# First batch computed in step with the weight loads over four output accumulators, with a second PSUM layout for the rest

## The chip, the cores and the metric

The kernel runs on one core of one Trainium2 chip. The metric is the time of one execution in device microseconds (us). Two spans appear: the time that a run reports, and the span of its trace, from the first to the last instruction, some 2 us shorter. Each run also has a mean granted TensorE clock, where 1.0 is full speed.

Most runs of the kernel before agree within one per cent. Runs carry a state, fast or slow; for one core "slow" means over 1.5% above the fastest run of the same kernel.

## The reference, cut to what matters

```python
B, H, S, Ns, D = (8, 8, 512, 32, 64)          # x: B,H,S,D   state: B,H,Ns,D
scores = scale * x @ state^T ; a = softmax(scores) ; xread = a @ state
scores2 = scale * state @ x^T ; a2 = softmax(scores2) ; sread = a2 @ x
y = concat([xread, sread], axis=2)            # per batch 512 + 32 rows
y = y.transpose(0, 2, 1, 3).reshape(B * 544, 512)
h = y @ w_in                                   # 512 -> 2048
out = (0.5 * h * (1 + erf(h / sqrt(2)))) @ w_out   # 2048 -> 512
```

There are eight batches. The kernel never forms `xread`: it multiplies the small `state` with `w_in` first (`pmat`), and then the transposed attention weights with that product (`mm1`).

## The kernel before: the parts that matter here

Engines run their own instruction lists, each in the order in which the kernel records them (e1 and e8 below show it: moving two recorded calls took back 15 us, and a product recorded behind sixteen load issues on POOL ran 11.5 us after its operand was ready). PE is TensorE (matmuls), DVE the vector engine, ACT the scalar engine, POOL the GpSimd engine (it also issues the large loads). Of PSUM, where matmuls write, the kernel uses eight banks: six for work in progress and two as accumulators, each of which gathers one output tile over several steps until DVE copies it out.

```python
ps_f = tile_pool(name="ps_f", bufs=6, space=PSUM)   # six banks of work
ps_o = tile_pool(name="ps_o", bufs=2, space=PSUM)   # two output accumulators
# loads on the POOL queue, in this order:
#   w_in 0, w_in 1, state 1..7, x 1, w_in 2, w_in 3, w_out 0, w_out 1, x 2, w_out 2, w_out 3, x 3

def norm(b, half):                   # softmax weights of a half batch: all on DVE
    nc.vector.reduce_sum(out=cs, in_=e4)        # waits for the Exp on ACT
    nc.vector.reciprocal(out=ics, in_=cs)
    nc.vector.tensor_tensor(out=A.a[...], in0=e4, in1=ics, op=mult)

def mm1(b, m):                       # first layer, one of 16 tiles of a batch
    hp = ps_f.tile([128, 512]); 2 matmuls (attention^T, P)
    nc.scalar.activation(out=gs[b][:, m, :], in_=hp, func=Gelu)

def evac(ps, rows):                  # accumulator -> SBUF -> HBM
    nc.vector.tensor_copy(out=osb, in_=ps)
    nc.sync.dma_start(out=rows, in_=osb)

def mm2(u):                          # second layer: a unit is 4 matmuls, 16 units per batch
    b, r = u // 16, u % 16
    if b == 0:  j, q = 2 * (r // 8) + r % 2, (r % 8) // 2     # two tiles side by side
    else:       j, q = r // 4, r % 4                          # one tile after the other
    if q == 0:  ops[j % 2] = ps_o.tile(...)
    4 matmuls (g of hidden blocks 4q..4q+3, w_out) added to the accumulator
    if q == 3:  evac(...)

def steady(b):                       # what is done for the next batch nb, by step s
    d[0] = begin, rearr, load_x, xtr(nb, 0) ; d[1] = xtr(nb, 1)
    d[3] = scores(nb, 0), scores(nb, 1), norm(nb, 0), norm(nb, 1)
    d[7] = pmat(nb, (0, 1)) ; d[9] = atr ; d[11], d[12] = sread ; d[13] = pmat ; d[14] = srt

lag = 16
for b in range(B):
    for s in range(16):
        for f in plan.get(s, ()): f()
        mm1(b, s); done += 1
        if done > lag: mm2(u); u += 1
```

`xtr` transposes x, `scores` makes the logits and their Exp, `atr` transposes the attention weights, `sread` and `srt` make the reads of the state rows.

The softmax here doesn't subtract the row's maximum and nothing guards it: scores larger than these inputs give would overflow.

Of the kernel before, what the change touches and what calls it, by code (L numbers as in the profile page):

```python
# [9 lines left out]
FP32 = mybir.dt.float32  # L10
# [7 lines left out]
def kernel(  # L18
# [8 lines left out]
    nc = tc.nc  # L27
# [13 lines left out]
    att = ctx.enter_context(tc.tile_pool(name="att", bufs=2))  # L41
    gpool = ctx.enter_context(tc.tile_pool(name="gpool", bufs=3))
    opool = ctx.enter_context(tc.tile_pool(name="opool", bufs=4))
    ps_f = ctx.enter_context(tc.tile_pool(name="ps_f", bufs=6, space=bass.MemoryType.PSUM))
    ps_o = ctx.enter_context(tc.tile_pool(name="ps_o", bufs=2, space=bass.MemoryType.PSUM))

    ctx.enter_context(tc.manual_schedule())



# [8 lines left out]
    st_f = persist.tile([128, 2, D], FP32, name="st_f")  # L59
    st_bf = persist.tile([128, B, 2, D], BF16, name="st_bf")  # L60
    x0f = persist.tile([128, 2, HC, SJ * D], FP32, name="x0f")
    warm = persist.tile([128, 512], BF16, name="warm")
    x4s = [persist.tile([128, SJ, HC, 132], BF16, name=f"x4_{i}") for i in range(2)]

# [2 lines left out]
    x0_rows = x[0].rearrange("(t c) (p j) d -> p t c (j d)", t=2, j=SJ)  # L67
    nc.scalar.dma_start(out=st_f, in_=st_rows[:, 0, :, :])
    for c in range(HC):
        eng = nc.sync if c % 2 == 0 else nc.scalar  # L70
        eng.dma_start(out=x0f[:, :, c, :], in_=x0_rows[:, :, c, :])

    make_identity(nc, ident)
    nc.vector.memset(warm, 0.0)  # L74
# [5 lines left out]
    def load_w_in(f):  # L80
        for t in range(2):
            nc.gpsimd.dma_start(
                out=w_in_bf[64 * t:64 * t + 64, :, f * 512:(f + 1) * 512],
                in_=moe_w_in[256 * t:256 * t + 256, f * 512:(f + 1) * 512].rearrange(
                    "(c d) f -> d c f", c=HC
                ),
            )
# [3 lines left out]
    def load_w_out(i):  # L91
        nc.gpsimd.dma_start(out=w_out_bf[:, 4 * i:4 * i + 4, :], in_=w_out_r[:, 4 * i:4 * i + 4, :])
# [3 lines left out]
    def load_x(b):  # L96
        xb = xin.tile([128, H, SJ * D], BF16, name="xb", tag="xb")
        nc.gpsimd.dma_start(out=xb, in_=x[b].rearrange("h (p j) d -> p h (j d)", j=SJ))
        xbs[b] = xb

    load_w_in(0)
    load_w_in(1)
    nc.gpsimd.dma_start(
        out=st_bf[:, 1:B, :, :].rearrange("q b t d -> q (b t) d"),
        in_=st_rows[:, 1:B, :, :].rearrange("q b t d -> q (b t) d"),
    )
    load_x(1)
    load_w_in(2)
    load_w_in(3)
    load_w_out(0)  # L110
    load_w_out(1)
    load_x(2)
    load_w_out(2)
    load_w_out(3)
    load_x(3)


    def keep_warm(n):
# [61 lines left out]
    def xtr0(c):  # L180
        A = atts[0]
        ps = ps_f.tile([128, SJ, 128], BF16, name="xT_ps", tag="f")
        for j in range(SJ):
            nc.tensor.transpose(ps[:, j, :], A.x4[:, j, c, 2:130], ident)
        nc.scalar.copy(out=A.xT[:, c, :, :], in_=ps)

    def xtr(b, half):
        A = atts[b]
# [6 lines left out]
    def score_mms(b, c):  # L195
        A = atts[b]
        if c % 2 == 0:
            A.pt = ps_f.tile([128, SJ, 2, 2, NS], FP32, name="pt", tag="f")
        for j in range(SJ):
            nc.tensor.matmul(  # L200
                A.pt[:, j, :, c % 2, :],
                lhsT=A.xT[:, c, j, :],
                rhs=sbd[:, b, c, :],
                start=True,
                stop=True,
            )
# [10 lines left out]
    def scores(b, half):  # L217
        score_mms(b, 2 * half)
        score_mms(b, 2 * half + 1)
        expo(b, half)  # L220

    def norm(b, half):
        A = atts[b]
        G = SJ * 2
        hs = slice(64 * half, 64 * half + 64)
        e4 = A.e[:, :, hs].rearrange("p g (c n) -> p g c n", n=NS)
        cs = att.tile([128, G, 2], FP32, name="cs", tag="cs")
        nc.vector.reduce_sum(out=cs, in_=e4, axis=AX.X)  # L228
        ics = att.tile([128, G, 2], FP32, name="ics", tag="ics")
        nc.vector.reciprocal(out=ics, in_=cs)  # L230
        nc.vector.tensor_tensor(  # L231
            out=A.a[:, :, hs].rearrange("p g (c n) -> p g c n", n=NS),
            in0=e4,
            in1=ics[:, :, :].to_broadcast((128, G, 2, NS)),
            op=ALU.mult,
        )
# [61 lines left out]
    def pmat(b, fs, act=()):  # L298
        if b not in Ps:
            Ps[b] = att.tile([128, 2, d_ff], BF16, name="P", tag="P")  # L300
        pss = []
        for f in fs:
            ps = [ps_f.tile([128, 512], FP32, name="p_ps", tag="f") for t in range(2)]
            for c in range(HC):
                for t in range(2):
                    nc.tensor.matmul(  # L306
                        ps[t][32 * c:32 * c + 32, :],
                        lhsT=sbd[64 * t:64 * t + 64, b, c, 32 * t:32 * t + 32],
                        rhs=w_in_bf[64 * t:64 * t + 64, c, f * 512:(f + 1) * 512],
                        start=True,  # L310
                        stop=True,
                    )
            pss.append(ps)
        for f, ps in zip(fs, pss):
            for t in range(2):
                dst = Ps[b][:, t, f * 512:(f + 1) * 512]
                if (f, t) in act:
                    nc.scalar.copy(out=dst, in_=ps[t])  # L318
                else:
                    nc.vector.tensor_copy(out=dst, in_=ps[t])  # L320
# [20 lines left out]
    def evac(ps, rows, last=False):  # L341
        osb = opool.tile([128, d_model], FP32, name="osb", tag="osb")
        if last:
            h = d_model // 2
            nc.vector.tensor_copy(out=osb[:, 0:h], in_=ps[:, 0:h])
            nc.sync.dma_start(out=rows[0][0][:, 0:h], in_=osb[:, 0:h])
            nc.scalar.copy(out=osb[:, h:], in_=ps[:, h:])
            nc.scalar.dma_start(out=rows[0][0][:, h:], in_=osb[:, h:])
            return
        nc.vector.tensor_copy(out=osb, in_=ps)  # L350
        for r, src in rows:
            nc.sync.dma_start(out=r, in_=osb[src, :])

    def mm2(u):
        b, r = u // 16, u % 16
        if b == 0:
            j, q = 2 * (r // 8) + r % 2, (r % 8) // 2
        else:
            j, q = r // 4, r % 4
        if q == 0:  # L360
            ops[j % 2] = ps_o.tile([128, d_model], FP32, name="op", tag="op")
        ps = ops[j % 2]
        for m in range(4 * q, 4 * q + 4):
            nc.tensor.matmul(  # L364
                ps,
                lhsT=gs[b][:, m, j * 128:(j + 1) * 128],
                rhs=w_out_bf[:, m, :],
                start=(m == 0),
                stop=(m == MC - 1),
            )  # L370
        if q == 3:
            rows = out[b * SB:b * SB + S, :].rearrange("(p j) n -> j p n", j=SJ)[j]
            evac(ps, [(rows, slice(0, 128))], last=(u == 16 * B - 1))

    def mm1_sr(m):
        hp = ps_f.tile([128, B * NS], FP32, name="hps", tag="f")
# [30 lines left out]
    for c in range(HC):  # L407
# [6 lines left out]
    expo(0, 0)  # L414
    xtr0(3)
    score_mms(0, 2)
    keep_warm(2)
    score_mms(0, 3)
    expo(0, 1)
    norm(0, 0)  # L420
    norm(0, 1)
    keep_warm(6)
    pmat(0, (0,), act=((0, 0), (0, 1)))
    keep_warm(4)
    atr(0)
    keep_warm(2)

    extra = {
        0: {
            1: [lambda: pmat(0, (1,))],  # L430
            3: [lambda: state_prep(1, B)],
            5: [lambda: begin(1), lambda: rearr(1), lambda: xtr(1, 0)],
            6: [lambda: xtr(1, 1), lambda: scores(1, 0), lambda: scores(1, 1)],
            7: [lambda: pmat(0, (2,))],
            8: [lambda: norm(1, 0), lambda: norm(1, 1)],
            10: [lambda: pmat(0, (3,))],
            12: [lambda: pmat(1, (0,))],
            13: [lambda: atr(1)],
            14: [lambda: pmat(1, (1,))],
        },  # L440
        1: {
            0: [lambda: sread(0, 0)],
            1: [lambda: sread(0, 1), lambda: pmat(1, (2,))],
            2: [lambda: srt(0)],
            3: [lambda: pmat(1, (3,))],
            4: [lambda: sread(1, 0)],
            5: [lambda: sread(1, 1), lambda: begin(2), lambda: rearr(2), lambda: load_x(4), lambda: xtr(2, 0)],
            6: [lambda: xtr(2, 1), lambda: srt(1)],
            8: [lambda: scores(2, 0), lambda: scores(2, 1), lambda: norm(2, 0), lambda: norm(2, 1)],
            10: [lambda: pmat(2, (0, 1), act=((0, 1), (1, 1)))],  # L450
            12: [lambda: atr(2)],
            13: [lambda: sread(2, 0)],
# [26 lines left out]
        d[14] = [lambda: srt(nb)]  # L479
        return d  # L480

    u = 0
    lag = 16
    done = 0
    for b in range(B):
        plan = extra[b] if b in extra else steady(b)
        for s in range(MC):
            for f in plan.get(s, ()):
                f()
            mm1(b, s)  # L490
            done += 1
            if done > lag:
                mm2(u)
                u += 1
# [40 lines left out]
```

## Time and profile before

| | before |
|---|---|
| time, median of 4 runs | 241.5 us (240.62 to 242.85) |
| span of the trace | 238.6 us |
| first `mm1`, first Gelu, first `mm2` | 14.73, 16.37, 31.91 us |
| period of one batch from batch 3 on (start of `srT` to start of `srT`) | 24.87 us |

The page of the kernel before. The first two lines are the span and the busy time of each engine with its share; then PE's busy tenths and its granted clock in 40 slices of 6 us; then the chain of waits that ended last, by engine.

```profile
span 238.6 us, 3733 instructions
...
PE 223.9 (94%) x1535; PEld 110.6 (46%) x1564; DVE 104.8 (44%) x198; ACT 124.9 (52%) x208; POOL 28.4 (12%) x41
...
PE   5996797989999999999999999999999999999993
...
PEclk9999999999999999999999999999999999999999
...
PE 89%; DVE 5%; DMA 2%; issue 1%; ACT 1%; ACTq 0%
```

PE is the limit nearly everywhere; only the first ten slices leave it idle. The waits of PE, in all, times, longest, from the same trace:

```profile
PE xT_ps L192 <- DVE x L168: 3.0, 2, 1.8
PE hp L330 <- DVE P L320: 1.5, 4, 0.8
PE xT_ps L184 <- DVE x L175: 1.4, 2, 1.1
```

None of these lies after 52 us.

### The profile page before, as it was taken

The numbers are of one execution on the slowest core, as the hardware profiler recorded it, in microseconds if no ns is written. First come the engines' busy times: TensorE is split into PE (matmuls) and PEld (weight loads), VectorE is DVE, ScalarE is ACT, GpSimd is POOL, SyncE is SP. The second block draws the span as 40 slices with busy tenths as digits, with TensorE's granted clock in tenths as the row PEclk, the third lists the DMA queues.
The fourth block names the chain that finished last, engine by engine and source line by source line (L and its number), as shares of the span: only waits on it lengthen the run. The fifth ranks groups of instructions, "written<-read, shape, count | busy, mean of one in ns | idle before, by whom it ended". The sixth has DMA issues, their size and how long they took to land.

```text
span 238.6 us, 3733 instructions
## 1 busy us (share of the span) xinstructions
PE 223.9 (94%) x1535; PEld 110.6 (46%) x1564; DVE 104.8 (44%) x198; ACT 124.9 (52%) x208; POOL 28.4 (12%) x41
## 2 busy tenths in 40 slices
PE   5996797989999999999999999999999999999993
PEld 1543243535544454444545454545454444557441
DVE  3646975574646433734283428343735112111120
ACT  2577742394486447745693559454945444335100
POOL 8745003103100400030002100000000000000000
PEclk9999999999999999999999999999999999999999
DMA  7999999720822180210111111111021111121022
GB/s 192 165 191 205 202 204 127 92 88 0 105 73 88 44 135 0 79 40 16 44 47 44 44 47 44 44 48 44 0 92 44 44 44 47 52 80 44 22 69 89
DMA packets 19889, 18.36 MB, mean 77 GB/s; under 512 B 3104, under 2 KB 15648, under 8 KB 19872
## 3 DMA queue, kind: packets, MB, share of 16 engines
q0 software_dynamic: 13376, 8.09, 24.7%
q1 hardware_dynamic: 5536, 9.31, 10.5%
q10 hardware_dynamic: 960, 0.72, 1.1%
q8 instruction: 12, 0.20, 0.3%
q14 instruction: 5, 0.04, 0.1%
HBM read 17.30 MB, written 8.91 MB: 110 GB/s over the span
## 4 chain that ended last, share of the span: by engine, by line
PE 89%; DVE 5%; DMA 2%; issue 1%; ACT 1%; ACTq 0%
PE op L364 46%; PE hp L330 22%; PE p_ps L306 4%; PE sr L264 3%; PE hps L378 3%; PE ops L390 3%; PE xT_ps L192 3%; DMA x0f<-in_x_dram 2%; PE warm_ps L121 2%; PE pt L200 2%; PE aT_ps L255 1%; DVE P L320 1%; DVE x L168 1%; DVE a L231 1%; DVE sbd L148 1%
## 5 line engine op out<-in xcount | busy, mean ns | idle before, releaser
L364 PE MATMUL op<-w_out_bf,g 128*128 128x512 bf16 x498 | 128.6, 379 | 1.0
L337 ACT ACTIVATE g<-hp 128x512 bf16<-128x512 f32 x128 | 73.9, 601 | 71.5 <-PE hp L330 67.7
L364 PEld LDWEIGHTS <-g 128*128 128x128 bf16 x512 | 50.0, 98 | 58.8
L330 PE MATMUL hp<-AT,P 128*128 128x512 bf16 x243 | 73.5, 380 | 2.7 <-DVE P L320 1.5
L350 DVE COPY osb<-op 128x512 f32<-128x512 f32 x31 | 21.4, 690 | 47.5 <-PE op L364 46.9
L330 PEld LDWEIGHTS <-P 128*128 128x128 bf16 x256 | 21.6, 97 | 24.9 <-issue 7.6
L320 DVE CAST P<-p_ps 128x512 bf16<-128x512 f32 x38 | 24.3, 684 | 8.1 <-PE p_ps L306 8.1
L168 POOL COPY x<-xb 128x1024 bf16<-128x1024 bf16 x10 | 10.4, 1042 | 96.1 <-PE sr L264 57.6
L228 DVE TENSOR_REDUCE cs<-e 128x16 f32<-128x512 bf16 x16 | 10.9, 682 | 22.9 <-ACT e L210 22.9
L318 ACT CAST P<-p_ps 128x512 bf16<-128x512 f32 x26 | 14.0, 590 | 7.1 <-PE p_ps L306 6.8
L193 DVE COPY xT<-xT_ps 128x1024 bf16<-128x1024 bf16 x14 | 9.6, 688 | 7.2 <-PE xT_ps L192 7.2
L306 PE MATMUL p_ps<-w_in_bf,sbd 64*32 64x512 bf16 x256 | 11.2, 383 | 0.5
L192 PE MATMUL xT_ps<-ident,x 128*128 128x128 bf16 x112 | 8.6, 220 | 3.0 <-DVE x L168 3.0
L231 DVE TENSOR_TENSOR a<-e,ics 128x512 bf16<-128x512 bf16 x16 | 11.1, 691 | 0.6
L210 ACT ACT_TABLE_LOAD x7 | 9.0, 1283 | 3.2 <-PE pt L200 3.2
L385 ACT ACTIVATE g_sr<-hps 128x256 bf16<-128x256 f32 x16 | 6.1, 383 | 8.4 <-PE hps L378 8.0
L192 PEld LDWEIGHTS <-x 128*128 128x128 bf16 x112 | 7.3, 98 | 6.7 <-DVE x L168 3.8
L337 ACT ACT_TABLE_LOAD x8 | 10.3, 1283 | 0.1
L264 PE MATMUL sr<-x,e 128*128 128x260 bf16 x64 | 10.0, 277 | 0.0
L273 DVE RECIPROCAL inv<-sr 128x1 f32<-128x1 f32 x16 | 2.6, 165 | 16.7 <-PE sr L264 16.6
L121 PE MATMUL warm_ps<-warm 128*128 128x512 bf16 x19 | 8.1, 564 | 1.2 <-DVE warm L74 1.2
L210 ACT ACTIVATE e<-pt 128x512 bf16<-128x512 f32 x16 | 8.8, 595 | 0.8 <-PE pt L200 0.7
(50 smaller groups left out, 117.3 us busy)
## 6 DMA issues: line engine op xcount, KB each, us to landing
out_dram<-osb SPq DMA_DIRECT2D x31, 256.0 KB, 2.3
xb<-in_x_dram POOLq DMA_DIRECT2D x7, 512.0 KB, 10.5
w_in_bf<-in_moe_w_in_dram POOLq DMA_DIRECT2D x8, 256.0 KB, 9.4
w_out_bf<-in_moe_w_out_dram POOLq DMA_DIRECT2D x4, 512.0 KB, 14.4
x0f<-in_x_dram SPq DMA_DIRECT2D x2, 256.0 KB, 3.3
x0f<-in_x_dram ACTq DMA_DIRECT2D x2, 256.0 KB, 4.8
out_dram<-osb SPq DMA_DIRECT2D x8, 64.0 KB, 1.7
st_bf<-in_state_dram POOLq DMA_DIRECT2D x1, 224.0 KB, 8.9
```

The lines of the kernel that those rows point to most:

```text
L121: nc.tensor.matmul(ps, lhsT=warm[:, 0:128], rhs=warm, start=True, stop=True)
L192: nc.tensor.transpose(ps[:, ci, j, :], A.x4[:, j, 2 * half + ci, 2:130], ident)
L210: nc.scalar.activation(out=A.e[:, :, 64 * half:64 * half + 64], in_=A.pt.rearrange("p j t c n -> p (j t) (c n)"), func=AF.Exp, scale=scale,)
L231: nc.vector.tensor_tensor(out=A.a[:, :, hs].rearrange("p g (c n) -> p g c n", n=NS), in0=e4, in1=ics[:, :, :].to_broadcast((128, G, 2, NS) ...
L264: nc.tensor.matmul(sr, lhsT=A.e[:, 2 * j + t, :], rhs=A.x4[:, j, :, 1 + 65 * t:66 + 65 * t], start=(j == 0), stop=(j == SJ - 1),)
L306: nc.tensor.matmul(ps[t][32 * c:32 * c + 32, :], lhsT=sbd[64 * t:64 * t + 64, b, c, 32 * t:32 * t + 32], rhs=w_in_bf[64 * t:64 * t + 64, c ...
L318: nc.scalar.copy(out=dst, in_=ps[t])
L320: nc.vector.tensor_copy(out=dst, in_=ps[t])
L330: nc.tensor.matmul(hp, lhsT=Ps[b][:, t, m * 128:(m + 1) * 128], rhs=atts[b].AT[:, t, :], start=(t == 0), stop=(t == 1),)
L337: nc.scalar.activation(out=gs[b][:, m, :], in_=hp, func=AF.Gelu)
L350: nc.vector.tensor_copy(out=osb, in_=ps)
L364: nc.tensor.matmul(ps, lhsT=gs[b][:, m, j * 128:(j + 1) * 128], rhs=w_out_bf[:, m, :], start=(m == 0), stop=(m == MC - 1),)
```

## The change

The intent: let batch 0 use each block of `w_in` and `w_out` as it lands, instead of running all its first-layer tiles before the first second-layer matmul at 31.9 us. For that batch 0 has four accumulators and four work banks; afterwards a second layout returns to six and two. The lag falls from 16 to 12, and with it the order of the second-layer units changes for all batches. The start is trimmed as well.

```diff
-    ps_f = ... bufs=6 ; ps_o = ... bufs=2
+    early = ExitStack()
+    ps_f = early ... "ps_f0", bufs=4 ; ps_o = early ... "ps_o0", bufs=4
...
-        eng = nc.sync if c % 2 == 0 else nc.scalar
-        eng.dma_start(out=x0f[:, :, c, :], in_=x0_rows[:, :, c, :])
+        nc.sync.dma_start(out=x0f[:, :, c, :], in_=x0_rows[:, :, c, :])
...
-    # loads: w_in 0, w_in 1, state, x 1, w_in 2, w_in 3, w_out 0, w_out 1, x 2, ...
+    # loads: w_in 0, w_out 0, w_in 1, then (load_rest, recorded after norm(0, 0)):
+    #        w_out 1, w_in 2, w_out 2, state, x 1, w_in 3, w_out 3, x 2, x 3
...  (batch 0: the copy of one xT goes to DVE; its scores and first pmat use ps_o)
+        eng = nc.gpsimd if b == 0 and half == 0 else nc.vector
+        eng.tensor_tensor(out=A.a[...], in0=e4, in1=ics, op=mult)
...
     def mm2(u):
         b, r = u // 16, u % 16
-        if b == 0: j, q = 2 * (r // 8) + r % 2, (r % 8) // 2
-        else:      j, q = r // 4, r % 4
+        if u >= 16 * B - 8: mm2_unit(b, r // 4, r % 4)
+        else:               mm2_unit(b, 2 * (r // 8) + r % 2, (r % 8) // 2)
...
+    nc.scalar.activation(out=gate, in_=hmask, func=AF.Gelu)   # loads the Gelu table early
     norm(0, 0)
+    load_rest()
     norm(0, 1)
-    keep_warm(6)
+    keep_warm(2)
...
+    group0(0, {2: [pmat(0, 1)]})        # 4 mm1, then 4 units of 4 mm2; mid-way the next pmat
+    group0(1, {2: [pmat(0, 2)]})
+    group0(2, {2: [state_prep(1, B)]})
+    begin(1); rearr(1); xtr(1, 0); xtr(1, 1); scores(1, 0); scores(1, 1)
+    pmat(0, 3); sread(0, 0)
+    group0(3, {0: [norm(1, 0), norm(1, 1), sread(0, 1), pmat(1, 0)],
+               1: [srt(0)], 2: [pmat(1, 1)], 3: [atr(1)]})
+    pmat(1, (2,))
+    early.close()
+    ps_f = ... bufs=6, reuse_waits="tile" ; ps_o = ... bufs=2, reuse_waits="tile"
...  (batch 1: pmat(1, 3) at step 1, x of batch 2 at steps 2 and 3, sread at 4 and 5,
...   scores and norms of batch 2 at 7; other steps as before)
-    u = 0 ; lag = 16 ; for b in range(B):
+    u = 16 ; lag = 12 ; for b in range(1, B):
```

More of the change, by code (lines that the diff above doesn't have):

```diff
@@ L43 @@
     opool = ctx.enter_context(tc.tile_pool(name="opool", bufs=4))
-    ps_f = ctx.enter_context(tc.tile_pool(name="ps_f", bufs=6, space=bass.MemoryType.PSUM))
-    ps_o = ctx.enter_context(tc.tile_pool(name="ps_o", bufs=2, space=bass.MemoryType.PSUM))
+    PSUM = bass.MemoryType.PSUM
     ctx.enter_context(tc.manual_schedule())
+    early = ExitStack()
+    ps_f = early.enter_context(tc.tile_pool(name="ps_f0", bufs=4, space=PSUM))
+    ps_o = early.enter_context(tc.tile_pool(name="ps_o0", bufs=4, space=PSUM))
     w_in_bf = persist.tile([128, HC, d_ff], BF16, name="w_in_bf")
@@ L61 @@
     x0f = persist.tile([128, 2, HC, SJ * D], FP32, name="x0f")
+    gate = persist.tile([128, HC], FP32, name="gate")
     warm = persist.tile([128, 512], BF16, name="warm")
@@ L101, with load_rest @@
     load_w_in(0)
+    load_w_out(0)
     load_w_in(1)
-    nc.gpsimd.dma_start(
-        out=st_bf[:, 1:B, :, :].rearrange("q b t d -> q (b t) d"),
-        in_=st_rows[:, 1:B, :, :].rearrange("q b t d -> q (b t) d"),
-    )
-    load_x(1)
-    load_w_in(2)
-    load_w_in(3)
-    load_w_out(0)
-    load_w_out(1)
-    load_x(2)
-    load_w_out(2)
-    load_w_out(3)
-    load_x(3)
+    def load_rest():
+        load_w_out(1)
+        load_w_in(2)
+        load_w_out(2)
+        nc.gpsimd.dma_start(
+            out=st_bf[:, 1:B, :, :].rearrange("q b t d -> q (b t) d"),
+            in_=st_rows[:, 1:B, :, :].rearrange("q b t d -> q (b t) d"),
+        )
+        load_x(1)
+        load_w_in(3)
+        load_w_out(3)
+        load_x(2)
+        load_x(3)
     def keep_warm(n):
@@ L184, in xtr0 @@
             nc.tensor.transpose(ps[:, j, :], A.x4[:, j, c, 2:130], ident)
-        nc.scalar.copy(out=A.xT[:, c, :, :], in_=ps)
+        if c < 3:
+            nc.scalar.copy(out=A.xT[:, c, :, :], in_=ps)
+        else:
+            nc.vector.tensor_copy(out=A.xT[:, c, :, :], in_=ps)
     def xtr(b, half):
@@ L197, in score_mms @@
         if c % 2 == 0:
-            A.pt = ps_f.tile([128, SJ, 2, 2, NS], FP32, name="pt", tag="f")
+            pool, tag = (ps_o, "op") if b == 0 else (ps_f, "f")
+            A.pt = pool.tile([128, SJ, 2, 2, NS], FP32, name="pt", tag=tag)
         for j in range(SJ):
@@ L230, in norm @@
         nc.vector.reciprocal(out=ics, in_=cs)
-        nc.vector.tensor_tensor(
+        eng = nc.gpsimd if b == 0 and half == 0 else nc.vector
+        eng.tensor_tensor(
             out=A.a[:, :, hs].rearrange("p g (c n) -> p g c n", n=NS),
@@ L302, in pmat @@
         for f in fs:
-            ps = [ps_f.tile([128, 512], FP32, name="p_ps", tag="f") for t in range(2)]
+            pool, tag = (ps_o, "op") if b == 0 and f == 0 else (ps_f, "f")
+            ps = [pool.tile([128, 512], FP32, name="p_ps", tag=tag) for t in range(2)]
             for c in range(HC):
@@ L352, in evac, with mm2_unit @@
             nc.sync.dma_start(out=r, in_=osb[src, :])
-    def mm2(u):
-        b, r = u // 16, u % 16
-        if b == 0:
-            j, q = 2 * (r // 8) + r % 2, (r % 8) // 2
-        else:
-            j, q = r // 4, r % 4
+    def mm2_unit(b, j, q):
         if q == 0:
-            ops[j % 2] = ps_o.tile([128, d_model], FP32, name="op", tag="op")
-        ps = ops[j % 2]
+            ops[b, j] = ps_o.tile([128, d_model], FP32, name="op", tag="op")
+        ps = ops[b, j]
         for m in range(4 * q, 4 * q + 4):
@@ L372, in mm2 @@
             rows = out[b * SB:b * SB + S, :].rearrange("(p j) n -> j p n", j=SJ)[j]
-            evac(ps, [(rows, slice(0, 128))], last=(u == 16 * B - 1))
+            evac(ps, [(rows, slice(0, 128))], last=(b == B - 1 and j == SJ - 1))
+    def mm2(u):
+        b, r = u // 16, u % 16
+        if u >= 16 * B - 8:
+            mm2_unit(b, r // 4, r % 4)
+        else:
+            mm2_unit(b, 2 * (r // 8) + r % 2, (r % 8) // 2)
     def mm1_sr(m):
@@ L416 @@
     score_mms(0, 2)
-    keep_warm(2)
     score_mms(0, 3)
     expo(0, 1)
+    nc.scalar.activation(out=gate, in_=hmask, func=AF.Gelu)
     norm(0, 0)
+    load_rest()
     norm(0, 1)
-    keep_warm(6)
+    keep_warm(2)
     pmat(0, (0,), act=((0, 0), (0, 1)))
@@ L425, with group0 @@
     atr(0)
-    keep_warm(2)
-    extra = {
-        0: {
-            1: [lambda: pmat(0, (1,))],
-            3: [lambda: state_prep(1, B)],
-            5: [lambda: begin(1), lambda: rearr(1), lambda: xtr(1, 0)],
-            6: [lambda: xtr(1, 1), lambda: scores(1, 0), lambda: scores(1, 1)],
-            7: [lambda: pmat(0, (2,))],
-            8: [lambda: norm(1, 0), lambda: norm(1, 1)],
-            10: [lambda: pmat(0, (3,))],
-            12: [lambda: pmat(1, (0,))],
-            13: [lambda: atr(1)],
-            14: [lambda: pmat(1, (1,))],
-        },
-        1: {
-            0: [lambda: sread(0, 0)],
-            1: [lambda: sread(0, 1), lambda: pmat(1, (2,))],
-            2: [lambda: srt(0)],
-            3: [lambda: pmat(1, (3,))],
+    def group0(f, mid):
+        for m in range(4 * f, 4 * f + 4):
+            mm1(0, m)
+        for j in range(SJ):
+            if j in mid:
+                for g in mid[j]:
+                    g()
+            mm2_unit(0, j, f)
@@ new lines @@
+    group0(0, {2: [lambda: pmat(0, (1,))]})
+    group0(1, {2: [lambda: pmat(0, (2,))]})
+    group0(2, {2: [lambda: state_prep(1, B)]})
+    begin(1)
+    rearr(1)
+    xtr(1, 0)
+    xtr(1, 1)
+    scores(1, 0)
+    scores(1, 1)
+    pmat(0, (3,))
+    sread(0, 0)
+    group0(3, {
+        0: [lambda: norm(1, 0), lambda: norm(1, 1), lambda: sread(0, 1), lambda: pmat(1, (0,))],
+        1: [lambda: srt(0)],
+        2: [lambda: pmat(1, (1,))],
+        3: [lambda: atr(1)],
+    })
+    pmat(1, (2,))
@@ L446 @@
+    early.close()
+    ps_f = ctx.enter_context(
+        tc.tile_pool(name="ps_f", bufs=6, space=PSUM, reuse_waits="tile")
+    )
+    ps_o = ctx.enter_context(
+        tc.tile_pool(name="ps_o", bufs=2, space=PSUM, reuse_waits="tile")
+    )
+    extra = {
+        1: {
+            1: [lambda: pmat(1, (3,))],
+            2: [lambda: begin(2), lambda: rearr(2), lambda: load_x(4), lambda: xtr(2, 0)],
+            3: [lambda: xtr(2, 1)],
             4: [lambda: sread(1, 0)],
-            5: [lambda: sread(1, 1), lambda: begin(2), lambda: rearr(2), lambda: load_x(4), lambda: xtr(2, 0)],
@@ L448 @@
-            6: [lambda: xtr(2, 1), lambda: srt(1)],
-            8: [lambda: scores(2, 0), lambda: scores(2, 1), lambda: norm(2, 0), lambda: norm(2, 1)],
+            5: [lambda: sread(1, 1)],
+            6: [lambda: srt(1)],
+            7: [lambda: scores(2, 0), lambda: scores(2, 1), lambda: norm(2, 0), lambda: norm(2, 1)],
             10: [lambda: pmat(2, (0, 1), act=((0, 1), (1, 1)))],
@@ L480, in steady @@
         return d
-    u = 0
-    lag = 16
+    u = 16
+    lag = 12
     done = 0
-    for b in range(B):
+    for b in range(1, B):
         plan = extra[b] if b in extra else steady(b)
```

## The prediction

> **What bounds it now.** The page: TensorE (PE) busy 94% of a 238.6 us span, full clock in all slices. The chain of waits that ended last is 89% PE; second-layer matmuls (L364) 46%, first-layer (L330) 22%. From about 62 us each batch takes 24.87 us (the sr matmuls recur at 78.74, 103.61, 128.48, 153.35), against about 24.65 of streaming PE work (96 matmuls of 512 columns at 0.216 us = 20.7, pmat 4 x 0.28, transposes, scores, reads of state). So the steady part has nothing to give; only the first 62 us have. There (timeline): first real mm1 at 14.73, first Gelu at 16.37 after a 1.28 us table load, first mm2 at 31.91, batch 2 begins at 61.86. Between 14.73 and 61.86 I count about 37.9 us of PE work, so 9.3 us of loss: some 6 while only 16 first-layer tiles are run before any mm2, 1.8 at 40.5 to 42.3 (xT waits for DVE), 1.0 at 51 (Gelu after two table loads).
>
> **What changes.**
> 1. Start. The gate Gelu takes the table load (1.28 us[...]) off the chain before the first Gelu; fewer warming matmuls stand before pmat and aT; one xT copy goes to DVE (0.43 instead of 0.58), half a product to POOL. First mm1 about 13.4 (-1.3), first Gelu about 14.0 (-2.4). x on SP alone: last chunk near 7.2 as now (7.28).
> 2. Weights in the order used. Landing intervals read from the trace: 256 KB each 1.27 us. Estimates: w_in/w_out pairs land 10.6/13.2, 15.7/18, 21/23.5, 30/32.6, x1 27.5 (now 17.6). Each stands ready just before PE asks.
> 3. Batch 0 is done in four groups of 4 mm1 + 16 mm2, 5.2 us of PE plus 0.3 to 0.45 of prep, losing about 0.4 each to the last Gelu (Gelus issue every 0.49). The third group ends at about 31.
> 4. Paid instead: batch 1's preparation, formerly hidden in that slack, stands in one block before group 3: x to xT to scores to Exp table to Exp to Gelu table. In the present trace that sequence takes 5.4 us (19.3 to 24.7), and with four PSUM buffers sread and mm1 wait for Exp. DVE then holds a backlog (P casts 0.6 each, norms 1.6 each, accumulator copies 0.6, AT, x of batch 2), 16 to 18 us of work from 29.5 on; PE waits for srm, AT(1), and at step 2 of batch 1 for x of batch 2 (about 2.5 us). Group 3 ends near 44.
> 5. Lag 12 starts anew in batch 1: twelve mm1 steps without mm2, with two table loads and Exps (3.7 us of ACT) among them, not covered: about 3 us at pmat(2).
> Sum: after loses about 12 to 13 us against 9.3, less 1.3 at the start: +2 by my count. As the count of chained waits is pessimistic (any slack is missed), I take +1. From batch 2 on nothing changes; the tail is the same.
>
> **On the critical path:** all of it is PE waiting in the first 62 us; the total PE work is unchanged (minus a few warming matmuls).
>
> **Time:** 242.5 us, 8 in 10 within 238 to 247. Faster by over 2%: 0.12; within: 0.76; slower: 0.12.
>
> **Signs.** First mm2 near 15 us; PE dense from 15 to 31; idle PE between 31 and 38 with Exp/Gelu table loads; AT and x copies on DVE releasing PE at 44 to 50; a PE wait for Gelu near 56 to 59; later batches still 24.87 apart.
>
> **Wrong if:** weights arrive later than estimated (queue refill held up behind the POOL product), then slower; or DVE backlog is short enough that batch 1's prep overlaps, then up to 5 us faster.

The page of the kernel before has 1283 ns as the mean of its fifteen loads at L210 and L337.

## More of the kernel before

Timeline of the kernel before, columns: start, duration, engine, line, operation, out<-in, count, idle time before it and who ended it.

```profile
69.04 0.69 DVE L228 TENSOR_REDUCE cs<-e 128x16 f32<-128x512 bf16 x1 [4.10 <-ACT e L210]
...
71.42 1.03 PE L364 MATMUL op<-w_out_bf,g 128*128 128x512 bf16 x4
71.66 0.69 DVE L231 TENSOR_TENSOR a<-e,ics 128x512 bf16<-128x512 bf16 x1
72.27 0.68 DVE L350 COPY osb<-op 128x512 f32<-128x512 f32 x1
72.38 0.63 PE L306 MATMUL p_ps<-w_in_bf,sbd 64*32 64x512 bf16 x16
...
73.38 0.81 PE L364 MATMUL op<-w_out_bf,g 128*128 128x512 bf16 x3
```

Already here an accumulator's copy (L350) starts only when the two norms of the next batch have ended on DVE. The tile had ended at 68.57 us. PE does not mind: the four units that follow, from 68.83 to 74.2 us, go to the other accumulator.

## The result, and the profile after

The time rose from 241.5 us to a median of 266.24 us (262.41 to 268.24, 4 runs). By the 1.5% rule two of the four runs count as slow (267.17 and 268.24 us); the two fast ones took 262.41 and 265.30 us. The ratio of the fast runs is 1.092, with a 95% interval of 1.079 to 1.106. Ratios here are the mean time of one kernel's fast runs over that of the other's in the same rounds, so not quite the ratio of the medians quoted. The forecast of 242.5 us, with a range of 238 to 247, was wrong.

The page of the changed kernel, the lines that answer to those shown of before:

```profile
span 263.2 us, 3720 instructions
...
PE 230.3 (88%) x1527; PEld 111.1 (42%) x1556; DVE 103.7 (39%) x198; ACT 124.7 (47%) x208; POOL 29.3 (11%) x42
...
PE   5799978496995999789995999599969999999994
...
PEclk9689999779998999979999999999999999999999
...
PE 71%; DVE 13%; ACT 8%; DMA 3%; issue 3%; POOL 1%; ACTq 0%; POOLq 0%; DVEq 0%
```

Two things are new. PE has a dip about every 28 us through the whole steady part (the 5s and 6s of its row, long after the first phase), and the granted clock falls several times. The waits of PE name the first:

```profile
PE op L372 <- DVE osb L363: 13.5, 5, 2.7
PE hp L343 <- DVE P L333: 2.9, 2, 2.7
PE srT L299 <- DVE srm L286: 1.6, 2, 1.0
PE p_ps L319 <- ACT g L350: 1.5, 1, 1.5
```

Five times PE stood still for 2.7 us before a second-layer matmul, until DVE had copied an accumulator. Before had no such wait. The first of the five, in the timeline of the changed kernel:

```profile
77.53 0.69 DVE L363 COPY osb<-op 128x512 f32<-128x512 f32 x1 [1.90 <-PE op L372]
...
78.22 1.03 PE L372 MATMUL op<-w_out_bf,g 128*128 128x512 bf16 x4
...
79.52 1.03 PE L372 MATMUL op<-w_out_bf,g 128*128 128x512 bf16 x4
79.72 0.69 DVE L239 TENSOR_REDUCE cs<-e 128x16 f32<-128x512 bf16 x1 [1.50 <-ACT e L221]
...
82.33 0.69 DVE L243 TENSOR_TENSOR a<-e,ics 128x512 bf16<-128x512 bf16 x1
82.94 0.68 DVE L363 COPY osb<-op 128x512 f32<-128x512 f32 x1
83.68 1.86 PE L372 MATMUL op<-w_out_bf,g 128*128 128x512 bf16 x4 [2.70 <-DVE osb L363]
```

The accumulator of the unit at 78.22 is complete at about 79.25 us. DVE idles until 79.72, because next in its list stand the norms, whose Exp is not there yet; it does both norms and copies the accumulator at 82.94. By then PE wants that bank: the unit at 79.52 took the other accumulator (copied at 77.53), and the one at 83.68 needs this one.

The second thing, the clock, by windows of the changed kernel (columns: window, its length, then busy time of PE, PEld, DVE, ACT and POOL with instruction counts, the granted clock, DMA share, GB/s):

```profile
7.93:14.76 6.83, 5.67 (x34) 2.53 (x34) 3.33 (x7) 3.96 (x7) 5.00 (x7) 0.50 1.21 195
48.89:55.72 6.83, 5.71 (x32) 2.59 (x32) 3.14 (x6) 1.79 (x3) 0.00 (x0) 0.50 0.04 14
83.03:86.44 3.41, 2.76 (x7) 0.99 (x7) 0.59 (x1) 0.04 (x2) 0.00 (x0) 0.50 0.20 77
```

In these windows PE runs at half speed, for 3.41 or 6.83 us, after time in which it was partly idle: the four second-layer matmuls at 83.68 us took 1.86 us together, those at 79.52 us 1.03. There was a fourth such stretch from 113.75 to 117.16 us, after the second of the five waits; the last three waits had none. The trace shows a difference between them. The changes of its clock lie at 7.93, 14.76, 48.89, 55.72, 83.03, 86.44, 113.75 and 117.16 us, which are 2, 10, 2, 8, 1, 8 and 1 times 3.41 us apart. Count the time in such steps. The two waits that half clock followed put 2.05 and 2.43 us of PE idle time into the one step before it; the other three fell across two steps, with at most 1.90 us in one. In the first phase no such border shows: the half clock at 48.89 us followed a step with 2.67 us of idle time, but that at 7.93 us one with 1.55. Why the clock falls is not shown. The kernel before has full clock from 12.5 us, where the records begin, to 237.8 us, in its last microsecond. (Ahead of its records, the weight loads of its warming matmuls from 10.36 to 11.64 us stand 0.43 us apart, as those at half clock from 84.06 to 86.19 us in the changed kernel do.)

Where the 24.5 us of span came from, by the starts of `srT` (the last prepared piece of each batch):

| | before | after | difference |
|---|---|---|---|
| `srT` of batch 2 | 60.47 | 71.15 | +10.7, of which 3.45 are four units that after has already done there |
| batch 2 to 3 | 23.58 | 27.79 | +4.2 (half clock in it) |
| batch 3 to 4 | 24.87 | 29.34 | +4.5 (half clock in it) |
| batch 4 to 5, 5 to 6, 6 to 7 | 24.86, 24.88, 24.87 | 27.73, 27.74, 27.73 | +2.9 each |
| `srT` of batch 7 to the end | 55.12 | 51.68 | -3.4, the four units back |

So 17.3 us came in the steady part and 10.7 - 3.45 = 7.2 us in the first phase. (3.45 us is 16 matmuls at 0.216 us, the spacing of these matmuls in the trace.)

### The profile page after: what moved, and what is told of

It is laid out like the page before. It is cut to its first block, busy times and chain, and to the rows that moved or that the text cites. A ratio compares the mean times of both kernels' runs of the same rounds, so it can differ in the third digit from the quotient of the medians.

```text
span 263.2 us, 3720 instructions
## 1 busy us (share of the span) xinstructions
PE 230.3 (88%) x1527; PEld 111.1 (42%) x1556; DVE 103.7 (39%) x198; ACT 124.7 (47%) x208; POOL 29.3 (11%) x42
## 4 chain that ended last, share of the span: by engine, by line
PE 71%; DVE 13%; ACT 8%; DMA 3%; issue 3%; POOL 1%; ACTq 0%; POOLq 0%; DVEq 0%
PE op L372 37%; PE hp L343 16%; PE p_ps L319 4%; ACT g L350 3%; DVE cs L239 3%; ACT L221 3%; PE xT_ps L202 3%; DMA w_in_bf<-in_moe_w_in_dram 3%; PE hps L393 3%; PE ops L405 3%; PE sr L276 2%; DVE P L333 2%; DVE osb L363 2%; DVE a L243 2%; ACT e L221 1%
## 5 line engine op out<-in xcount | busy, mean ns | idle before, releaser
L372 PE MATMUL op<-w_out_bf,g 128*128 128x512 bf16 x497 | 130.1, 383 | 14.8 <-DVE osb L363 13.5
L363 DVE COPY osb<-op 128x512 f32<-128x512 f32 x31 | 21.4, 689 | 48.9 <-PE op L372 48.9
L343 PEld LDWEIGHTS <-P 128*128 128x128 bf16 x256 | 22.6, 99 | 27.1 <-issue 10.0
L319 PE MATMUL p_ps<-w_in_bf,sbd 64*32 64x512 bf16 x256 | 13.2, 411 | 3.0 <-ACT g L350 1.5
L202 PE MATMUL xT_ps<-ident,x 128*128 128x128 bf16 x112 | 9.3, 232 | 1.6 <-DVE x L175 1.5
L243 DVE TENSOR_TENSOR a<-e,ics 128x512 bf16<-128x512 bf16 x15 | 10.4, 692 | 0.5
L202 PEld LDWEIGHTS <-x 128*128 128x128 bf16 x112 | 7.9, 105 | 5.8 <-DVE x L175 2.9
L221 ACT ACT_TABLE_LOAD x7 | 9.0, 1283 | 2.7 <-PE pt L211 2.7
L350 ACT ACT_TABLE_LOAD x7 | 9.0, 1283 | 0.1
L268 DVE COPY AT<-aT_ps 128x1024 bf16<-128x1024 bf16 x7 | 4.8, 690 | 10.4 <-PE aT_ps L267 10.4
L319 PEld LDWEIGHTS <-sbd 64*32 64x32 bf16 x256 | 2.9, 90 | 13.0 <-issue 11.9
```

Source lines behind the costliest of these rows:

```text
L202: nc.tensor.transpose(ps[:, ci, j, :], A.x4[:, j, 2 * half + ci, 2:130], ident)
L221: nc.scalar.activation(out=A.e[:, :, 64 * half:64 * half + 64], in_=A.pt.rearrange("p j t c n -> p (j t) (c n)"), func=AF.Exp, scale=scale,)
L243: eng.tensor_tensor(out=A.a[:, :, hs].rearrange("p g (c n) -> p g c n", n=NS), in0=e4, in1=ics[:, :, :].to_broadcast((128, G, 2, NS)), op= ...
L319: nc.tensor.matmul(ps[t][32 * c:32 * c + 32, :], lhsT=sbd[64 * t:64 * t + 64, b, c, 32 * t:32 * t + 32], rhs=w_in_bf[64 * t:64 * t + 64, c ...
L343: nc.tensor.matmul(hp, lhsT=Ps[b][:, t, m * 128:(m + 1) * 128], rhs=atts[b].AT[:, t, :], start=(t == 0), stop=(t == 1),)
L350: nc.scalar.activation(out=gs[b][:, m, :], in_=hp, func=AF.Gelu)
```

## The experiments

Twelve kernels ran; all gave correct results. They ran in three sets of rounds, e1 to e4, e5 to e8 and e9 to e12, each with the kernel before but not with the changed kernel, so differences of a microsecond or two between sets are uncertain. Theory Q says that the steady loss is the accumulator copy queued behind the norms on DVE, made visible by the paired unit order at lag 12 with two accumulators. Its rivals are B (two accumulators are simply too few for pairs) and C (the half clock, or something in the new start, is the cause).

### Putting the norms one step later

```diff
-        d[3] = [scores(nb, 0), scores(nb, 1), norm(nb, 0), norm(nb, 1)]
+        d[3] = [scores(nb, 0), scores(nb, 1)]
+        d[4] = [norm(nb, 0), norm(nb, 1)]
```

> Only edit to the changed kernel: from batch 2 on, the two softmax norms of the next batch are recorded one step later (step 4 instead of 3), so on the in-order DVE the copy of the second accumulator of a pair (unit 7 of a batch) stands before the norms instead of behind them. Theory Q (the PE stall of 2.70 us that comes five times, at 83.7, 112.8, 142.1, 169.8 and 197.6 us, is an accumulator copy queued behind norms that wait for Exp): those five stalls go, batches recur every 24.9 us instead of 27.7 to 29.3, time about 248 to 250 us, i.e. 17 us less than the 266. Rival B (two accumulators are too few when both of a pair end one after the other, whatever stands on DVE): the stall stays at 2 us or more, time 260 or more. Rival C (the lost time is the half clock after the idle, of itself): the stalls stay.

The three timed fast runs took 247.41, 248.83 and 250.21 us; the ratio to before is 1.034. Moving two recorded calls took back 15 us between the means of the fast runs (17 us between the medians), as theory Q said, and the time is the one expected. The profiled execution of this kernel was a freak of 592.98 us in which all matmuls were slow (see the last section), so its trace could not be used for the waits; the kernels e5 to e7, which contain the same edit, have profiles, and none has a PE wait for `osb`. In e5 `srT` of batch 2 and of batch 7 start 123.06 us apart, exactly as in the kernel before; in the changed kernel it was 140.33. So the edit gives back the whole 17.3 us of the steady part.

### Before's unit order, or the old lag

```diff
 (e2_old_order)
-        if u >= 16 * B - 8: mm2_unit(b, r // 4, r % 4)
-        else:               mm2_unit(b, 2 * (r // 8) + r % 2, (r % 8) // 2)
+        mm2_unit(b, r // 4, r % 4)
 (e3_lag16)
-    lag = 12
+    lag = 16
```

> Only edit to the changed kernel: after batch 0 the second-layer units go in the order of the kernel before (one output tile of a batch at a time) at the new lag of 12. Theory Q: an accumulator is asked for again only four units after its neighbour ended, so the copy behind the norms is covered; the five 2.70 us stalls go; instead unit 3 needs the Gelu of the first-layer tile just issued (about 1 us per batch). Time about 249 to 254 us. Rival B and C: no better than 262.

> Only edit to the changed kernel: lag 16 instead of 12, order as changed. Theory Q: units 6 and 7 then fall at steps 6 and 7, three steps after the norms; the 2.70 us stalls go or fall under 1 us; the ramp of batch 1 has four more first-layer tiles without second-layer units, costing 1 to 2 us. Time about 249 to 252 us. Rival B: pairs still end together, stall stays, 262 or more.

They took 250.69 us and 247.09 us (ratios 1.040 and 1.026), with the norms where they were. Neither profile has a PE wait for `osb` (the 2.7 us that both still list is the one wait at the opening of the second layout, see below). Rival B fails here: both keep two accumulators, and e3 keeps the pairs. It is the distance between the end of a tile, the norms and the next use of that bank that counts. In e2 the batches recur every 25.09 us, so the extra cost of the old order was 0.2 us per batch, not about 1. In time e3 came out better than expected, but its ramp of batch 1 was not free: against e5 below, whose first `mm1` starts within 0.1 us of e3's, its profiled span is 2.2 us longer, all of it before batch 3.

### The suspected cause put into the kernel before

```diff
-        if b == 0: j, q = 2 * (r // 8) + r % 2, (r % 8) // 2
+        if u < 16 * B - 8: j, q = 2 * (r // 8) + r % 2, (r % 8) // 2
         else:      j, q = r // 4, r % 4
-    lag = 16
+    lag = 12
```

> The kernel before with two edits only: the paired order of the second-layer units for all batches but the last two tiles, and lag 12 instead of 16. Nothing of the new start, of the load order, or of the two PSUM layouts. Theory Q: the stall of about 2.7 us behind the norms appears here also, in batches 2 to 6 and perhaps 1, with some half-clock windows after it; time about 255 to 260 us instead of 241.5. Rival (the loss comes from the new start, the weights' order or the second PSUM layout): 239 to 244 us.

It took 260.65 us (259.61 to 260.85), ratio 1.083. Its waits of PE begin with the same line as those of the changed kernel, five times and in the same length:

```profile
PE op L364 <- DVE osb L350: 13.5, 5, 2.7
PE xT_ps L192 <- DVE x L168: 3.9, 2, 2.1
```

Without anything of the new start, the load order or the two layouts, these two lines of the change cost 19 to 20 us. This run also has four stretches of half clock, three of them after such a wait (mean clock 0.974 over 258.3 us, where four stretches of 3.41 us make 0.974). So rival C, as the source of the steady loss, falls: the half clock came once a wait had begun (in the changed kernel at 83.03 us in the wait from 80.98, and at 113.75 after the one that ended at 112.76), and batches 4 to 7 of the changed kernel lose 2.9 us each at full clock.

### Four accumulators to the end

```diff
-    early.close()
-    ps_f = ... bufs=6 ... ; ps_o = ... bufs=2 ...
+    # the first layout, 4 work banks and 4 accumulators, stays
```

> The changed kernel with the first PSUM layout (4 banks of work, 4 accumulators) kept to the end; norms, order and lag as changed, so the accumulator copies stand behind the norms as before. Theory Q in full (the stall needs both: a copy queued behind the norms AND no other free accumulator): the five 2.70 us stalls go although the DVE order is unchanged, and the 2.67 us wait at the opening of the second layout too; with 4 instead of 6 work banks the pmat pairs, which take 4 banks, wait for Gelu or casts, 0.5 to 1.5 us per batch: 246 to 254 us. Rival (the copy on DVE holds PE in some other way): stalls stay, 262 or more.

It took 253.83 us, ratio 1.046. The DVE order is that of the changed kernel, yet the wait for `osb` is gone, so both halves of theory Q are needed: a copy behind the norms, and no free bank. The wait at the opening of the second layout went too, as expected: the first `mm1` of batch 1 waits 0.88 us, for the attention copy. The price of four work banks is small and steady; this is its largest group of waits of PE (total, times, longest), with one of 0.5 us in each steady batch:

```profile
PE hp L343 <- ACT P L331: 3.8, 10, 0.5
```

Its batches recur every 26.06 us (between `srT` of batches 4, 5, 6 and 7) instead of 24.87. Not all of that difference is in listed waits; the rest stays open.

### Warming matmuls, and the opening of the second layout

e5 and e6 each add one edit to e1; e7 has both.

```diff
 (e5_norm_warm)
     score_mms(0, 2)
+    keep_warm(2)
     score_mms(0, 3)
...
-    keep_warm(2)
+    keep_warm(6)
     pmat(0, (0,), ...)
 (e6_norm_p12)
-    pmat(1, (2,))
     early.close()
...
-            1: [pmat(1, (3,))],
+            1: [pmat(1, (2,)), pmat(1, (3,))],
```

> The changed kernel with the norms one step later (e1_norm_later, 249 us) plus the warming matmuls of the kernel before put back at the start (2 between the last score tiles, 6 instead of 2 before the first pmat). Theory H (fewer warming matmuls let the PE fall to half clock from 7.9 to 14.8 us, which delays the first first-layer matmul): granted clock 1.0 up to the first mm1, first mm1 a microsecond earlier (13.3 to 13.8 instead of 14.5), time 1 to 1.5 us less than e1, about 247.5. Rival (start is bound by the arrival of the weights and of x, the clock does not matter): first mm1 still at 14.2 or later, time as e1 within 0.5.

> The changed kernel with the norms one step later plus one edit: the third pmat of batch 1 is recorded after the second PSUM layout is opened instead of just before. Theory S (the first first-layer matmul of batch 1, at 48.83 us, waits 2.67 us because its bank in the new layout is held until the DVE has cast that pmat, behind other copies): the wait at the opening falls by about 1.3 us (it then ends with the attention copy and the last accumulator copy, about 47.6), the half clock after it (48.9 to 55.7) gets shorter or goes; time 1.5 to 4 us less than e1, about 246 to 247.5. Rival (that matmul is held by the DVE backlog whatever the layout, the same copies follow anyway): wait moves to the next matmul, time as e1 within 1 us.

> The three edits together on the changed kernel (norms later, warming matmuls back, third pmat of batch 1 after the second layout). If the pieces add up: 244.5 to 247 us; still not under the 240.8 of the kernel before, as the start of batch 1's ramp without second-layer work (12 steps) and the preparation block of batch 1 remain.

| kernel | median, us | ratio to before (95%) | first `mm1`, us | clock before it, in the profiled run |
|---|---|---|---|---|
| e5_norm_warm | 246.80 | 1.024 (1.020 to 1.028) | 13.47 | full from 10.3, where its records begin |
| e6_norm_p12 | 244.11 | 1.013 (1.008 to 1.017) | 13.68 | half from 7.63 to 14.45 |
| e7_all | 244.58 | 1.016 (1.011 to 1.022) | 14.44 | full from 12.2, where its records begin |

Theory S holds: e7 differs from e5, of the same rounds, by this edit alone, and its median is 2.2 us lower. e6 is even 4.7 us under e1's 248.8, more than expected, but e1 ran in other rounds, so that size is uncertain. In the changed kernel the first `mm1` of batch 1 waited 2.67 us for a `pmat` cast; in e6 it waits 1.22 us for the attention copy instead:

```profile
PE hp L343 <- DVE AT L268: 1.2, 1, 1.2
```

The half clock from 48.9 to 55.7 us is gone from e6's profiled run as well. How much this adds is not shown; and the half clock does not hang on the 2.67 us wait alone, for e10, which waits 0.88 us there, has half clock from 47.6 to 54.4 us. The kernel language's detail by which the new pool holds that matmul back was not traced; the run shows only that it goes with the `pmat` recorded just before.

Theory H is not supported. e5 by itself met its forecast (13.47 and 246.80 us), but e7, with warm matmuls and full clock, was no faster than e6 without. The first `mm1` differs by up to a microsecond between profiled runs of kernels with equal starts (13.56 in e3, 14.50 in the changed kernel), so one look cannot settle it; whether e5's 2 us against e1 is the warming or chance stays open, as e1 and e5 ran in different rounds.

### The new start alone, in the kernel before

```diff
 (e8_before_start)  x of batch 0 on the SP queue; xT copy 3 on DVE; gate activation; and
+        eng = nc.gpsimd if b == 0 and half == 0 else nc.vector
 (e9_before_start_dve)  the same without this line
```

> The kernel before with only the new start: x of batch 0 on the SP queue alone, the Gelu table loaded early by the gate activation, one xT copy on DVE and half a product on POOL; warming matmuls, load order, lag, unit order and PSUM layout as before. Theory (start gains what the prediction said): first Gelu at about 14.7 to 15.2 instead of 16.37, but the first phase then waits for weights and for the DVE, so the time is 0.5 to 2 us less than before: 239 to 240.5 us. Rival (the start is hidden behind the weights): 240.5 to 241.5.

> As e8_before_start but with the product of the first norm left on DVE. In e8 that product stood on POOL behind fourteen load issues that wait for earlier loads; it ran at 21.85 us and held the first attention transposes by 9.41 us. Theory P (that queueing is the whole loss of e8; the rest of the new start is a gain): attention transposes at about 13 us, first Gelu at 14.5 to 15.3, time 239 to 241 us. Rival (x on one queue or the early table load costs by itself): 243 us or more.

e8 missed badly: 251.79 us, ratio 1.044. The reason is again an in-order list. In the kernel before, all loads are recorded on POOL ahead of the norm, so the product waited behind sixteen load issues (e9's expectation says fourteen; it is sixteen in the trace), several of which wait for earlier loads to land. Timeline and waits of e8:

```profile
20.95 0.88 POOL L98 DMA_DIRECT2D xb<-in_x_dram  x1 [0.55 <-DMA w_in_bf<-in_moe_w_in_dram]
21.85 1.06 POOL L235 TENSOR_TENSOR a<-e,ics 128x512 bf16<-128x512 bf16 x1
22.97 1.03 PE L249 MATMUL aT_ps<-ident,a 128*128 128x128 bf16 x8 [9.41 <-POOL a L235]
```

In the change itself the product is safe, at 9.76 us, because `load_rest` is recorded after it. e9 settles what the rest of the start is worth: 240.93 us, ratio 0.998 (0.994 to 1.003), so nothing measurable. Its first Gelu came at 15.16 instead of 16.37 us, but its PE then waited 1.84 us for x of batch 1 where before waited 1.27, and its `srT` of batch 0 started at 35.18 against 34.97. The gain is given back there, well before the steady part.

### The rest of the first phase

After e6 some 2.6 us were missing to before. e11 starts from e1 and reorders batch 1's preparation against the DVE backlog; e12 adds second-layer units to the gap in which ACT changes tables.

```diff
 (e11_reorder, on e1)
-        1: [srt(0)], 2: [pmat(1, 1)], 3: [atr(1)]
+        1: [atr(1), srt(0)], 2: [pmat(1, 1)]
-    pmat(1, (2,))                       # before the second layout
...
-            1: pmat(1, 3);  2: begin(2), rearr(2), load_x(4), xtr(2, 0);  3: xtr(2, 1)
-            4: sread(1, 0);  5: sread(1, 1);  6: srt(1)
+            1: pmat(1, 2);  2: begin(2), rearr(2), load_x(4), sread(1, 0)
+            4: xtr(2, 0);  5: xtr(2, 1);  6: sread(1, 1);  8: pmat(1, 3), srt(1)
 (e12_fill, on e11)
-            if done > lag:
+            if (7 <= s <= 10) if b == 1 else done > lag:
                 mm2(u); u += 1
```

> The changed kernel with norms later, and the work of batch 1 recorded in another order: its attention transposes before the read of state in the last group of batch 0, its third pmat in step 1 of batch 1, x of batch 2 transposed in steps 4 and 5 instead of 2 and 3 (its copy on DVE in step 2), reads of state of batch 1 in steps 2 and 6. Theory D (what is left over before, 3 us after e6, is PE waiting for the DVE backlog: 1.2 us for the attention copy at 46.3, 2.5 us for x of batch 2 at 50.5 in e6): these two waits fall below 1 us together, time 241 to 243 us against 244.1 of e6. Rival (the backlog only moves to the next wait): 243.5 or more.

> e11_reorder plus: the first four second-layer units of batch 1 go at its steps 7 to 10, where in e6 PE waits 2 us for Exp and Gelu after the two table loads, instead of steps 12 to 15. Theory R (the ramp without second-layer work is uncovered ACT time): the waits of 0.5 and 1.5 us at 57.9 and 60.3 in e6 go; 1 to 2 us less than e11: 239.5 to 241.5 us, at or just under the kernel before. Rival: as e11 within 0.5 us.

e11 took 245.18 us, ratio 1.016: the backlog only moved, as its rival said. The attention wait went, the wait for x of batch 2 fell from 2.5 to 0.9 us, but a `pmat` now waits 0.8 us for an `osb` copy, the ACT waits stayed, and the profiled run has half clock from 59.9 to 63.4.

e12 took 240.46 us (239.35 to 241.05), ratio 0.995 (0.991 to 0.9995), 4.7 us less than e11 where 1 to 2 were expected. In e11 the two waits for Exp and Gelu were 1.16 and 1.32 us. In e12 the second is gone and the first is 0.30 us; 2.2 us are thus accounted for. The half clock after them is gone too (3.41 us at half speed is at most 1.7 us of lost work). The page of e12:

```profile
PE   5899988889999999999999999999999999999993
...
PEclk9999999999999999999999999999999999999998
```

The dips in the steady part are gone and the clock is whole. This version is level with the kernel before, at best half a per cent under it; it beats the change by 23.6 us between the means of the fast runs. It shows that the idea of the change costs nothing when its order is right, and also that it gains next to nothing.

## Why the prediction was wrong

The step that failed is the sentence "From batch 2 on nothing changes; the tail is the same", with its sign "later batches still 24.87 apart". They were 27.73 to 29.34 us apart. I read the diff of `mm2` as a regrouping of the same PE work, which it is (96 matmuls per batch as before), and did not ask what else stands on DVE between the end of a tile and the next use of its bank. Before, unit 3 ends a tile at step 3, behind the norms too (its copy at 72.27), but its bank is wanted again only at unit 8. After, units 6 and 7 end a pair at steps 2 and 3, the norms are recorded in step 3 ahead of unit 7's copy, and unit 9 wants that bank two steps later. The runs show that the order on DVE and the number of banks act together: five bubbles of 2.70 us, cured by order (e1, e2), by lag (e3) or by banks (e10).

Point by point:

- What bounds the kernel: right. PE, 94% busy, and a steady part with nothing to give.
- The weights' order: right. Both halves of `w_in` 0 to 3 had landed by 11.07, 16.18, 21.28 and 30.51 us (estimates 10.6, 15.7, 21 and 30), x of batch 1 at 28.17 (27.5). PE waited only 0.5 us for a weight.
- The start: right in mechanism, too large in size. The first Gelu came at 15.50, not 14.0; e9 shows that even a gain of 1.2 us there does not reach the end.
- Groups of batch 0: right within 2 us. The first `mm2` came at 16.59 (near 15 predicted), and the third group ended near 33 (31), partly because everything began a microsecond later.
- Batch 1's block and the DVE backlog: right in kind. PE waited for srm (1.0), for x of batch 2 (1.1, predicted about 2.5), and at `pmat(2)` for Exp and Gelu (0.5 and 1.5, predicted 3). Missing was the 2.67 us at the opening of the second layout, which e6 showed to hang on the `pmat` recorded just before it; the wait for the attention copy that was predicted does not show beside it (in e6, without the 2.67 us, it is 1.22).
- The clock was counted as full throughout, since before had it so. The stretches of half clock at 7.9 and 48.9 us were not foreseen. With the waits they make the first phase 7.2 us longer, where the count said 2; how much is due to each was not separated.
- The forecast then took half of its own count, on the ground that such counts are pessimistic. It was optimistic: a count of known waits leaves out those not thought of.

That the time is near the sum is shown by putting things back, with ratios to the kernel before: 1.092 for the change, 1.034 with the norms later (e1), 1.013 with the `pmat` moved as well (e6), and 0.995 in e12.

## What to carry to other kernels

When a change alters the order or the lag of work that rotates through a few buffers, list for each buffer who frees it, what stands ahead of that instruction on its in-order engine, and how many steps later the buffer is wanted again; an engine that is 40% busy can still be the one that frees too late. Record the short instruction that frees a buffer ahead of the long ones that wait for something else, and never put a compute instruction behind load issues that wait for landings (in e8 that held PE for 9.41 us). Count an idle gap of PE like those here as longer than it looks: half clock followed two of the five gaps of 2.70 us in the changed kernel, and three of five in e4.

## What else the traces showed

- Gaps of 2.70 us, in matmul work that was otherwise dense, were followed by half clock in two of five cases, and it began at 83.03 us, inside the gap that ended at 83.68. At the start of the changed kernel half clock came at 7.93 us although no single wait of PE from 2 to 8 us was longer than 1.1 us. The four executions of the changed kernel took 262.41, 265.30, 267.17 and 268.24 us at mean clocks of 0.984, 0.961, 0.961 and 0.958; why the clock differs from one execution to the next is not shown.
- One execution of e1 took 592.98 us with PE 98% busy, without any clock record; the second-layer matmuls took 834 ns each by the profile, against 379 ns before, for the whole run. Their starts lie 0.62 us apart (median, against 0.216 us), 2.9 times as far. What slowed them is not shown:

```profile
L372 PE MATMUL op<-w_out_bf,g 128*128 128x512 bf16 x512 | 331.6, 834 | 0.0
```

- A change of ACT's table, in the one looked at, cost the load, 1.28 us, and next to nothing more: in the kernel before, Exp ran to 50.01, the load began at 50.02, and Gelu began at 51.32. A switch cost 1.3 us.
- On POOL, compute that was recorded behind load issues which wait for earlier loads came late: the product in e8 ran at 21.85 us, 11.5 us after its operand was ready at 10.3.
